# A new written order for five engines: the transposes of the second x0 half ahead of K's matmuls on the second kb slice, and the orders behind it

## The chip, the core and the metric

The kernel runs on one core of a Trainium2 chip. A core has TensorE (PE; its weight loads are shown apart as PEld), VectorE (DVE), ScalarE (ACT), GpSimd (POOL) and SyncE (SP), which here only issues DMAs. Each engine runs its own list of instructions in order, and the lists meet through semaphores. The metric is the device time of one execution in microseconds, median over runs. A profile is one execution; its span runs from the first to the last instruction of the program.

## What is computed

A gated sum of two branches over x of 2048 rows and 512 columns, in bf16. Branch a is attention with 32 heads of 16 columns, in four segments of 512 rows, with a running memory M, z that each segment reads and then extends. Branch b is a gated MLP with 1792 hidden columns.

```python
g = _sigmoid((x * gate_w).sum(-1, keepdims=True))
# branch a, segment s
logits = jnp.einsum('bhqd,bhkd->bhqk', qs, ks) * scale + mask
a_dot = jnp.einsum('bhqk,bhkd->bhqd', _softmax(logits), vs)
pq = phi(qs)
a_mem = num(pq, M) / den(pq, z)
o = sig_beta * a_mem + (1.0 - sig_beta) * a_dot
M, z = M + phi(ks).T @ vs, z + phi(ks).sum()
# branch b
h = _gelu(x @ w_gate) * (x @ w_up)
out = g * (o @ wo) + (1 - g) * (h @ w_down)
```

## The kernel before

The kernel is built from 1290 tasks, each a few instructions on one engine. The function `_build` makes them, `Sched.schedule` puts them in the order that the table `ORDER` (line 43) writes out for each engine, name by name, and `Emitter` adds the semaphore waits that follow from reads and writes. So the order on every engine is written by hand, or rather by a search that ran elsewhere, and the choice of engine for a task that can run on ScalarE or on VectorE is made by the list in which its name stands. `schedule` also walks through the lists with estimated durations, and from that it only takes which of the four PSUM banks psW0 to psW3 a group of matmuls gets (`Grp`, `bank_free`); `LANDING` (line 39) holds the landing times that it assumes for the first loads. Estimates don't change an order.

What the names mean, for segment s (0 to 3) and tile t:

- `x0t0a_u`, `x0t0b_u`, `x0t1_u`: the first segment's x comes in two halves u (`x0_0`, `x0_1`, 256 KB each, by SP) and is transposed on TensorE (line 645): two transposes, two, and four for each half. `x0ev...` copies them out of PSUM into xT (lines 652 and 653).
- `K0_t.i`: eight matmuls of 256 columns each, one task each, with i = 0 and 1 on the first x half with the first two slices of wk (`w_wk0`, `w_wk1`, 128 KB each, by ACT's queue), 2 and 3 the same on the second half, 4 to 7 with `w_wk2`. In this order `K0_t.0` needs wk0, `K0_t.1` needs wk1, and `.2` and `.3` need the second x half.
- `Q`, `V`, `G` (gate), `U` (up), `D` (down and output projection) with `s_t.0` and `.2`: two matmuls of 512 columns each, into a bank of psW. `Kev`, `Qev`, `Vev`, `Gev` copy a finished bank out (line 563 on ScalarE, 566 on VectorE). Q of segment 0 uses the banks of psXALL instead. `R` are the D matmuls of segments 0 to 2 cut into four row tiles that run side by side.
- `kp`, `kl`: copies of K masked for two interleaved heads (kpad, klow; lines 777, 786, 763, 765).
- `qk s_t A0 B0 L A1 B1`: logits of four heads at a time into all four banks of psXALL (line 928); `exp` (line 934, ScalarE) reads all four, so the next qk waits for the exp and the next exp for the qk. `msk` (line 937, GpSimd) cuts off the masked part. There are 18 of these a segment, and the other work of TensorE stands between them, about five pairs of matmuls a gap.
- `pv`, `pvt`, `norm`: the product with V in column tiles, its transpose on VectorE (line 990), and four or five steps that divide and write oT (lines 1002 to 1010).
- `pke`, `pkc`, `pqe`, `pqc`: phi of K and of Q, an exp on ScalarE (line 745) and two steps on VectorE (748, 750). `pkT` are DMA transposes of phi(K), `mz`, `mzacc`, `mzbd` (lines 894 to 913) bring the memory up to date; `numx`, `num`, `numd`, `nump`, `numl` read it; `oTd` are DMA transposes of the result.
- `gelu` (lines 1048 and 1059), `Um` (line 1075, the product with up), `fin` (lines 1123 and 1125, the scaled output) and `out`, its DMA. `gmul`, `gsum`, `gexs`, `gts`: the gate g of a segment; a gsum on ScalarE is line 813.

A run of tasks between two qk that has a `pv` in it is put into column tiles as a whole (`Sched.column_runs`): each matmul there is four instructions that run side by side.

The order on TensorE around the change:

```python
"... x0t0a_0 x0t0b_0 x0t1_0 K0_2.0 K0_3.0 K0_0.0 K0_1.0 K0_0.1 x0t0a_1 "
"K0_3.1 x0t0b_1 x0t1_1 K0_1.1 K0_2.1 K0_3.2 K0_2.2 K0_1.2 K0_2.3 ..."
```

## Time and profile before

| what | us |
|---|---|
| median of 3 runs | 262.89 |
| lowest, highest | 262.35, 263.35 |
| the profiled execution | 262.34 |
| its span, first to last instruction | 261.1 |
| TensorE busy | 256.8 |
| ScalarE busy | 210.6 |
| VectorE busy | 186.7 |
| GpSimd busy | 106.1 |

The granted clock of TensorE is 1.0 in this execution. In the rows, a group has its line in the kernel, engine, operation, the tile written and those read, the shape and how often; then the start and the length, or the busy time and the mean of one. In square brackets stands how long the engine had been idle before it and what ended that. SPq and ACTq are DMA issues of those engines.

### The profile page before, as it was taken

Reading aid. Unit: us, or ns where it says so; the run is one execution under the profiler, and the core shown is the slowest. Engines: PE = TensorE matmul, PEld = TensorE weight load, DVE = VectorE, ACT = ScalarE, POOL = GpSimd, SP = SyncE. Lnnn points to the kernel's source line nnn. Section 1 sums busy time; section 2 is a strip of 40 time slices with the busy share of each in tenths; the row PEclk is TensorE's granted clock in tenths of the full one; section 3 lists DMA queues with packets and bytes.
Section 4 is the critical chain, followed back from the end, with each engine's and each line's share of the span. In section 5 each row is a group of like instructions: output and inputs, shape, how many; then the busy total and the mean of one; then the engine's idle time right before and its main releaser. Section 6 shows DMA issues by size and latency. Waiting matters only on the chain.

```text
span 261.1 us, 10363 instructions
## 1 busy us (share of the span) xinstructions
PE 256.8 (98%) x4646; PEld 126.6 (48%) x4646; DVE 186.7 (71%) x350; ACT 210.6 (81%) x187; POOL 106.1 (41%) x260
## 2 busy tenths in 40 slices
PE   7999999999999999999999999999999999999996
PEld 3644445345544664534554563554455444453454
DVE  1598988998999238999986115999999502598743
ACT  3789898999999988789877788888975877776722
POOL 8316574923001873163650217352280053436420
DMA  6951338922126744110005113302000300310002
GB/s 220 316 171 22 64 64 237 312 24 83 24 22 149 102 98 65 32 54 3 3 9 124 36 22 81 86 7 82 0 6 11 72 5 0 85 43 3 3 3 83
DMA packets 33100, 18.43 MB, mean 71 GB/s; under 512 B 21152, under 2 KB 32800, under 8 KB 33056
## 3 DMA queue, kind: packets, MB, share of 16 engines
q1 hardware_dynamic: 32224, 16.99, 27.8%
q8 instruction: 36, 0.59, 1.0%
q10 hardware_dynamic: 832, 0.79, 0.9%
q14 instruction: 8, 0.07, 0.1%
HBM read 9.84 MB, written 2.10 MB: 46 GB/s over the span
## 4 chain that ended last, share of the span: by engine, by line
PE 93%; DVE 3%; DMA 2%; issue 1%; ACT 0%; DVEq 0%
PE psW L543 35%; PE psW L545 25%; PE psW L1096 14%; PE psXALL L928 8%; PE psW L976 5%; DMA wk<-in_A_wk_dram 2%; PE psXALL L545 2%; PE psW L984 1%; PE psXALL L543 1%; PE psXALL L847 1%; PE psW L894 1%; DVE tb L990 1%; DVE phq L750 0%; DVE obf L1006 0%; DVE hT L566 0%
## 5 line engine op out<-in xcount | busy, mean ns | idle before, releaser
L934 ACT ACTIVATE pt<-psXALL 128x2048 bf16<-128x2048 f32 x64 | 120.1, 1876 | 24.7 <-PE psXALL L928 21.9
L937 POOL TENSOR_SCALAR_AFFINE_SELECT pt<-pt 128x256 bf16<-128x256 bf16 x128 | 58.6, 470 | 92.6 <-ACT pt L934 88.1
L1075 DVE TENSOR_TENSOR hT<-psW,hT 128x512 bf16<-128x512 f32 x56 | 37.0, 683 | 7.2 <-PE psW L543 5.3
L937 POOL TENSOR_SCALAR_AFFINE_SELECT ptl<-ptl 128x512 bf16<-128x512 bf16 x32 | 22.1, 689 | 45.0 <-ACT ptl L934 43.2
L1096 PE MATMUL psW<-wd,hT 32*128 32x512 bf16 x576 | 35.0, 374 | 0.0
L543 PE MATMUL psW<-xT,wu 128*128 128x512 bf16 x118 | 29.4, 381 | 0.1
L545 PE MATMUL psW<-xT,wg 128*32 128x512 bf16 x464 | 27.8, 380 | 0.0
L990 DVE STREAM_TRANSPOSE tb<-psW 128x512 f32<-128x512 f32 x32 | 22.5, 707 | 6.6 <-PE psW L984 6.5
L543 PE MATMUL psW<-xT,wg 128*128 128x512 bf16 x108 | 26.3, 380 | 0.3 <-DVE hT L566 0.3
L545 PE MATMUL psW<-xT,wu 128*32 128x512 bf16 x424 | 26.0, 380 | 0.0
L928 PE MATMUL psXALL<-qT,kpad 32*128 32x320 bf16 (+3 forms) x512 | 25.7, 272 | 0.2 <-ACT ptl L934 0.2
L1125 DVE TENSOR_SCALAR ost<-psW,omgt 128x512 bf16<-128x512 f32 x10 | 7.4, 748 | 23.3 <-PE psW L543 21.6
L1096 PEld LDWEIGHTS psW<-wd,hT 32*128 32x128 bf16 x576 | 18.8, 93 | 10.6
L1059 ACT ACTIVATE hT<-psW 128x512 bf16<-128x512 f32 x28 | 15.6, 598 | 7.6 <-PE psW L545 7.5
L928 PEld LDWEIGHTS psXALL<-qT,kpad 32*128 32x128 bf16 x512 | 8.6, 92 | 23.1 <-ACT pt L934 16.0
L976 PE MATMUL psW<-pt,vaug 128*17 128x192 bf16 (+3 forms) x512 | 19.3, 273 | 0.0
L934 ACT ACTIVATE ptl<-psXALL 128x2048 bf16<-128x2048 f32 x8 | 15.1, 1882 | 2.7 <-PE psXALL L928 2.6
L543 PEld LDWEIGHTS psW<-xT,wu 128*128 128x128 bf16 x118 | 10.1, 98 | 13.7 <-issue 2.7
L976 PEld LDWEIGHTS psW<-pt,vaug 128*17 128x17 bf16 x512 | 12.1, 91 | 9.4 <-issue 0.8
L545 PEld LDWEIGHTS psW<-xT,wg 128*32 128x32 bf16 x464 | 11.3, 97 | 10.5 <-issue 0.6
L834 POOL COPY exsT<-exs 32x4 f32<-32x4 f32 x64 | 14.1, 220 | 5.2 <-ACT exs L824 1.5
L543 PEld LDWEIGHTS psW<-xT,wg 128*128 128x128 bf16 x108 | 10.0, 98 | 12.7 <-issue 0.6
(124 smaller groups left out, 382.5 us busy)
## 6 DMA issues: line engine op xcount, KB each, us to landing
out_dram<-ost SPq DMA_DIRECT2D x15, 128.0 KB, 1.9
wg<-in_B_w_gate_dram SPq DMA_DIRECT2D x2, 896.0 KB, 7.2
wu<-in_B_w_up_dram SPq DMA_DIRECT2D x2, 896.0 KB, 6.6
...
hT<-in_A_x_dram SPq DMA_DIRECT2D x2, 256.0 KB, 3.5
...
```

What stands on the lines that cost most here:

```text
L543: return e.matmul(view(), lhsT, rhs, start=first, stop=last)
L545: r = e.matmul(view()[c:c + 32, :], lhsT[:, c:c + 32], rhs, start=first, stop=last, tile_position=(0, c))
L834: cross = task(f"exsT{s}", POOL, [Instr(lambda e, g=g, c=c: e.tensor_copy(exsT[sl][32 * g:32 * g + 32, c:16:4], exs[32 * c:32 * c + 32, s4 ...
L928: instrs.append(Instr(lambda e, g=g, lhs=lhs, rhs=rhs, c0=c0, ncol=ncol: e.matmul(X[g][:, c0:c0 + ncol], lhs(32 * g), rhs(32 * g), start=T ...
L934: exp_task(s, f"exp{s}_{t}{name}", [Instr(lambda e: e.activation(dst[:], XALL[:, :].rearrange("p (g c) -> p g c", g=4), ACTF.Exp, scale=AT ...
L937: task(f"msk{s}_{t}{name}", POOL, [Instr(lambda e, view=view, pat=pat, base=base: e.affine_select(out=view, in_=view, compare_op=ALU.is_ge ...
L976: instrs.append(Instr(lambda e, t=t, q=q, kb=kb, slot=slot, c0=c0: e.matmul(gp.f32()[32 * q:32 * q + 17, 128 * kb + 64:512], Vaug[sl][:, k ...
L990: task(f"pvt{s}_{t}_{j}", DVE, [Instr(lambda e: e.transpose(Tb[:, j, :], gp.f32()[:, :]), [gp.key], [("Tb", j)], 0.71)], grp=gp)
L1059: lambda e, g=g, ft=ft, s=s: e.activation(hT[s % 2][:, ft, :], g.f32()[:, :], ACTF.Gelu_apprx_tanh),
L1075: task(f"Um{s}_{ft}", DVE, [Instr(lambda e, g=g, ft=ft: e.tensor_tensor(hT[sl][:, ft, :], g.f32()[:, :], hT[sl][:, ft, :], ALU.mult), [g.k ...
L1096: return Instr(lambda e: e.matmul(gs[tile].f32()[:, :], a[32 * r:32 * r + 32, :], b[32 * r:32 * r + 32, :], start=False, stop=False, tile_ ...
L1125: DVE: [Instr(lambda e: e.tensor_scalar(ost[:], g.f32()[:, :], omgt[:, gt:gt + 1], None, ALU.mult), rd, wr, dve_t(512, ap=True))]}, grp=g))
```

## The change

Only the two tables differ. In `LANDING`, x0_0 goes from 3.95 to 3.8 and w_wk1 from 5.3 to 5.7. In `ORDER`, all tasks are the same, but they stand in another order on every engine behind the first few, and 44 of those that can run on either of ScalarE and VectorE change the engine: 24 go to ScalarE, 20 to VectorE. In segment 0 these are 13 and 9.

```diff
 LANDING = {
-    "x0_0": 3.95, "w_wk0": 4.15, "x0_1": 5.2, "w_wk1": 5.3, "w_wk2": 6.6, ...
+    "x0_0": 3.8, "w_wk0": 4.15, "x0_1": 5.2, "w_wk1": 5.7, "w_wk2": 6.6, ...
...
     "pe": (
-        "warm0 ... x0t0a_0 x0t0b_0 x0t1_0 K0_2.0 K0_3.0 K0_0.0 K0_1.0 K0_0.1 x0t0a_1 "
-        "K0_3.1 x0t0b_1 x0t1_1 K0_1.1 K0_2.1 K0_3.2 K0_2.2 K0_1.2 K0_2.3 K0_1.3 K0_0.2 K0_2.4 K0_0.3 K0_1.4 K0_2.5 "
-        "K0_0.4 K0_3.3 K0_3.4 K0_1.5 K0_0.5 K0_0.6 K0_0.7 K0_2.6 K0_1.6 Q0_0.0 K0_1.7 Q0_1.0 K0_2.7 Q0_2.0 Q0_3.0 "
-        "Q0_0.2 Q0_1.2 K0_3.5 K0_3.6 Q0_3.2 Q0_2.2 K0_3.7 G0_2.0 G0_2.2 qk0_0A0 V0_3.0 V0_1.0 V0_1.2 V0_3.2 V0_0.0 "
+        "warm0 ... x0t0a_0 x0t0b_0 x0t1_0 K0_2.0 K0_3.0 K0_0.0 K0_1.0 x0t0a_1 x0t0b_1 "
+        "x0t1_1 K0_2.1 K0_3.1 K0_0.1 K0_1.1 K0_2.2 K0_3.2 K0_1.2 K0_0.2 K0_2.3 K0_1.3 K0_2.4 K0_0.3 K0_1.4 K0_2.5 "
+        "K0_0.4 K0_3.3 K0_3.4 K0_1.5 K0_0.5 K0_0.6 K0_2.6 K0_0.7 K0_1.6 K0_2.7 K0_1.7 Q0_3.0 Q0_0.0 Q0_1.0 Q0_1.2 "
+        "Q0_0.2 Q0_2.0 Q0_3.2 Q0_2.2 K0_3.5 K0_3.6 K0_3.7 G0_2.0 G0_3.0 qk0_0A0 G0_2.2 V0_2.0 V0_3.0 V0_3.2 V0_2.2 "
...
-        "qk0_2L G0_10.2 G1_3.0 G1_4.0 G1_4.2 G1_3.2 qk0_2A1 G0_1.0 G1_0.0 G0_1.2 G1_0.2 K1_3.0 qk0_2B1 G0_11.0 K1_3.2 "
+        "mz0 qk0_2L G0_0.0 V1_3.0 G1_4.0 G1_4.2 G0_0.2 qk0_2A1 G1_3.0 G1_3.2 V1_3.2 G0_10.0 G0_10.2 qk0_2B1 G0_11.0 "
...
     "act": (
-        "tload w_wk0 w_wk1 w_wq0 w_wv0 x0ev0b_0 x0ev0b_1 x0ev1_1 K0_0even K0_0ev K0_1ev pke0_0 kl0_11 Q0_1ev Q0_3ev "
-        "K0_3ev exp0_0A0 Vev0_1 gexp exp0_0B0 Vev0_0 Vev0_2 exp0_0L kl0_30 exp0_0A1 Vev1_1 exp0_0B1 pke0_1 exp0_1A0 "
+        "tload w_wk0 w_wk1 w_wq0 w_wv0 x0ev0b_0 x0ev0b_1 x0ev1_1 K0_0even K0_1ev K0_2ev kl0_01 pke0_0 Q0_1ev Q0_0ev "
+        "Q0_3ev kl0_10 K0_3ev exp0_0A0 gexp Vev0_3 exp0_0B0 gsum0_1 kl0_20 exp0_0L Vev0_0 exp0_0A1 Gev0_7 exp0_0B1 "
...
-        "exp1_2B0 exp1_2L K2_1ev exp1_2A1 exp1_2B1 pqe2_1 exp1_3A0 gsum2_1 exp1_3B0 gsum2_0 gsum2_2 exp1_3A1 Vev2_3 "
+        "exp1_2A0 Vev2_0 fin0_3 exp1_2B0 Q2_2ev exp1_2L pqe2_1 exp1_2A1 exp1_2B1 exp1_3A0 K2_0ev exp1_3B0 gsum2_3 "
+        "gsum2_0 gsum2_2 exp1_3A1 Vev2_3 gexs2 exp1_3B1 gelu2_0 gelu2_1 gelu2_2 gelu2_3 gelu2_4 gelu2_5 gelu2_6 "
...
     "dve": (
-        "x0ev0a_0 x0ev0a_1 x0ev1_0 kl0_01 K0_2ev kl0_10 Q0_0ev kp0_0 kl0_00 Q0_2ev Gev0_2 kp0_1 gmul0 kl0_31 Vev0_3 "
+        "x0ev0a_0 x0ev1_0 x0ev0a_1 K0_0ev kp0_0 kl0_21 kp0_1 Q0_2ev gmul0 Gev0_2 gsum0_2 kl0_11 Vev0_2 kl0_00 gsum0_3 "
...
-        "Gev1_9 pqc1_0 pvt0_1_0 mzacc0 Gev0_10 pvt0_1_1 mzbd0 Gev1_3 pqc1_1 Gev0_1 norm0_1 K1_3ev Gev0_11 gmul1 "
+        "pvt0_1_1 pvt0_1_0 mzacc0 pqc1_1 norm0_1 Vev1_3 Gev0_10 gmul1 Gev0_1 gsum1_0 gsum1_1 gsum1_2 mzbd0 K1_3ev "
...
     "pool": (
-        "ident masks vones consts msk0_0B0 msk0_0A0 omg msk0_0L msk0_0B1 msk0_0A1 exsT0 msk0_1A1 msk0_1B0 msk0_1A0 "
+        "ident masks vones msk0_0B0 msk0_0A0 msk0_0L msk0_0A1 msk0_0B1 exsT0 omg msk0_1A1 msk0_1A0 msk0_1B1 msk0_1B0 "
...
     "sp": (
-        "x0_0 x0_1 w_wk2 w_wq1 w_wv1 w_wg0 x1_0 w_gwb x1_1 w_beta x1_2 x1_3 w_wg1 Vlo0_0 gl10 gl11 gl00 gl01 pkT0_0 "
-        "Vlo0_1 pkT0_2 pkT0_1 pkT0_3 x2_3 x2_2 w_wu1 xt1 w_wu0 w_wd0 x2_0 x2_1 w_wo Vlo1_1 oTd1_2 oTd1_3 oTd1_1 w_wd1 "
+        "x0_0 x0_1 w_wk2 w_wq1 w_wv1 w_wg0 x1_0 w_gwb x1_1 w_beta x1_2 x1_3 w_wg1 gl00 gl11 Vlo0_1 gl10 gl01 pkT0_1 "
+        "pkT0_0 Vlo0_0 pkT0_2 pkT0_3 xt1 x2_3 x2_0 w_wu0 x2_1 w_wd0 w_wu1 w_wd1 x2_2 w_wo oTd1_0 x3_2 oTd1_1 oTd1_2 "
```

In the last segments the lists move in the same way: D1_3.16 goes behind qk2_1A1, fin1_0 from ScalarE to VectorE, and at the end ScalarE has fin3_1 and VectorE fin3_2 and fin3_0, where ScalarE had fin3_0 and fin3_2 and VectorE fin3_1.

More of the change, by code (lines that the diff above doesn't have):

```diff
@@ L39 @@
 LANDING = {
-    "x0_0": 3.95, "w_wk0": 4.15, "x0_1": 5.2, "w_wk1": 5.3, "w_wk2": 6.6, "w_wq0": 7.0, "w_wq1": 8.4, "w_wv0": 9.2,
+    "x0_0": 3.8, "w_wk0": 4.15, "x0_1": 5.2, "w_wk1": 5.7, "w_wk2": 6.6, "w_wq0": 7.0, "w_wq1": 8.4, "w_wv0": 9.2,
     "w_wv1": 10.2, "w_wg0": 12.2, "x1_0": 12.9, "w_gwb": 13.2, "x1_1": 13.8, "w_beta": 14.1, "x1_2": 14.4, "x1_3": 14.8,
```

147 rows, old and new, of the table ORDER are left out of this document.

## The prediction

> **What bounds the kernel now.** I read the shares of the page first, then the busy time by stretches of the span, then the chain of waits, and last the rows around its few waits.
>
> ```profile
> PE 256.8 (98%) x4646; PEld 126.6 (48%) x4646; DVE 186.7 (71%) x350; ACT 210.6 (81%) x187; POOL 106.1 (41%) x260
> PE 93%; DVE 3%; DMA 2%; issue 1%; ACT 0%; DVEq 0%
> ```
>
> ```profile
> 4.00:21.50 17.50, 16.71 (x146) 8.70 (x143) 11.59 (x25) 13.39 (x19) 7.44 (x19) 1.00 0.81 231
> 21.50:58.70 37.20, 36.92 (x589) 16.61 (x588) 33.92 (x62) 33.98 (x31) 22.29 (x55) 1.00 0.54 125
> 58.70:203.00 144.30, 144.26 (x2843) 72.73 (x2843) 111.06 (x213) 123.97 (x114) 54.20 (x134) 1.00 0.24 50
> 203.00:258.60 55.60, 55.23 (x1044) 27.10 (x1046) 29.76 (x52) 37.43 (x24) 19.35 (x40) 1.00 0.10 25
> ```
>
> The columns of the stretches are: length, then busy time of PE, PEld, DVE, ACT and POOL, then clock, DMA share and GB/s. TensorE is the bound in every stretch: it idles 0.79 us (17.50 less 16.71), then 0.28, 0.04 and 0.37, together 1.48 us between 4 and 258.6 us. Ends of matmuls are modelled, so gaps under some 0.27 us hide in "busy"; but what an order can win is of the size of 1.5 us, 0.6% of the time. VectorE (33.92 of 37.20) and ScalarE (33.98) are close behind in the second stretch: there a task put on the wrong one of the two can cost TensorE time.
>
> The 0.79 us has two parts at the start:
>
> ```profile
> 4.61 0.61 PE L543 MATMUL psW<-xT,wk 128*128 128x256 bf16 x4 [0.21 <-DVE xT L653]
> 5.80 0.27 PE L543 MATMUL psW<-xT,wk 128*128 128x256 bf16 x1 [0.58 <-DMA wk<-in_A_wk_dram]
> 5.91 0.27 PE L645 MATMUL psXALL<-ident,hT 128*128 128x128 bf16 x2
> 6.02 0.27 PE L543 MATMUL psW<-xT,wk 128*128 128x256 bf16 x1
> 6.13 0.50 PE L645 MATMUL psXALL<-ident,hT 128*128 128x128 bf16 x6
> 6.46 2.51 PE L543 MATMUL psW<-xT,wk 128*128 128x256 bf16 x21
> ```
>
> K0_0.1 stands ahead of the transposes of the second half of x0 and waits for wk1, so the transposes wait with it. The second wait that shows is at 48.43 us:
>
> ```profile
> 45.07 0.72 DVE mzbd L913
> 46.31 0.42 DVE phq L748
> 46.76 1.02 DVE phq L750
> 47.77 0.61 DVE hT L566
> 48.43 0.61 PE psW L543 x2
> ```
>
> These are steps of the chain of waits: G0_11.0 needs one of the four psW banks, and the copy that frees it (L566, Gev0_1) stands on VectorE behind mzbd0 and pqc1_1, both of which took long.
>
> **The head.** The order of the DMA issues at the start is unchanged, so the landings stay where they were.
>
> ```profile
> 1.27 0.42 SPq L580 DMA_DIRECT2D hT<-in_A_x_dram  x1
> 1.73 0.43 SPq L580 DMA_DIRECT2D wk<-in_A_wk_dram  x1
> ```
>
> ```profile
> hT<-in_A_x_dram SPq DMA_DIRECT2D x1, 256.0 KB, 4.1
> wk<-in_A_wk_dram SPq DMA_DIRECT2D x1, 256.0 KB, 5.3
> ```
>
> ```profile
> 1.29 4.37 DMA wk<-in_A_wk_dram
> ```
>
> x0's second half lands at 1.27 + 4.1 = 5.4 us, wk1 at 1.29 + 4.37 = 5.66, wk2 at 1.73 + 5.3 = 7.0. The diff puts all eight transposes of that half (x0t0a_1, x0t0b_1, x0t1_1) ahead of K0_2.1. They can start at 5.46 instead of 5.91. Six of them took 0.50 us with a last one of 0.22 (rows above), 0.056 us apart, so eight take 0.45 us and end at 5.91. The four matmuls K0_t.1 then issue back to back, 0.11 us each (21 in 2.51 - 0.27 us, the rows of 6.46), to 6.35. The same work was over at 6.72 before (both remaining K0_t.1 after 6.46, and a small gap). That is 0.37 us sooner. VectorE's copies follow: x0ev1_0 now stands before x0ev0a_1, but its transposes are done at 4.4, so it runs in the idle time before 5.3 and delays nobody. Then K0_2.4 needs wk2: six matmuls stand ahead of it, so TensorE is there at 6.35 + 6 x 0.11 = 7.01, against the landing at 7.0 plus the 0.13 us from landing to matmul that wk1 shows (5.66 to 5.80): 0.12 us back. What TensorE carries on is 0.25 us.
>
> In a sentence that the sum doesn't need: the Trainium skill, TensorE: Matmul & The Clock Gate, PE-mode transpose, says that transposes do not count as busy for the clock gate and stay at half rate; by that the eight would take 0.45 us more and the head would be about 0.1 us slower than before. The rows above deny it here: 0.056 us apart right behind an idle 0.58 us, at clock 1.00.
>
> **What ScalarE makes of the head.** The next consumer is exp0_0A0, behind these:
>
> ```profile
> 8.86 0.69 ACT L734 ACTIVATE kpad<-psW,maskc 128x512 bf16<-128x512 f32 x1 [1.36 <-PE psW L543]
> 9.57 1.09 ACT L563 ACTIVATE kT<-psW 128x512 bf16<-128x512 f32 x2
> 10.69 1.06 ACT L745 ACTIVATE pex<-kT 128x1024 bf16<-128x1024 bf16 x1
> 11.65 0.57 ACT L763 ACTIVATE klow<-kT,maskc 128x256 bf16<-128x256 bf16 x1
> 12.09 1.05 ACT L563 ACTIVATE qT<-psXALL 128x512 bf16<-128x512 f32 x2
> 13.03 0.59 ACT L563 ACTIVATE kT<-psW 128x512 bf16<-128x512 f32 x1
> 14.22 1.88 ACT L934 ACTIVATE pt<-psXALL 128x2048 bf16<-128x2048 f32 x1 [0.59 <-PE psXALL L928]
> 16.81 1.88 ACT L934 ACTIVATE pt<-psXALL 128x2048 bf16<-128x2048 f32 x1
> ...
> 47.58 0.60 ACT L563 ACTIVATE hT<-psW 128x512 bf16<-128x512 f32 x1
> ```
>
> ```profile
> 18.95 0.41 PE L928 MATMUL psXALL<-qT,klow 32*128 32x64 bf16 x32
> ...
> 21.56 0.40 PE L928 MATMUL psXALL<-qT,kpad 32*128 32x448 bf16 x8
> ```
>
> Before, ScalarE had 0.59 us to spare there. Now its list ahead of exp0_0A0 is K0_0even, three copies that were two (K1, K2 for K0, K1), kl0_01, pke0_0, three copies of Q that were two, kl0_10, K0_3ev: from start to start 0.71 + 2 x 0.50 + 0.48 + 0.96 + 3 x 0.48 + 0.44 + 0.50 = 5.5 us. K0_0even follows K0_0.7, which is eleven matmuls behind K0_2.4 (7.13 + 11 x 0.11 = 8.33; before it was 18 behind the one at 6.46, 8.48), so it starts 0.15 us sooner, at 8.71, so exp0_0A0 starts at 14.2: where it was. TensorE reaches qk0_0A0 at 13.51 for 13.77, but the next qk0_0B0 writes the same four psXALL banks and waits for exp0_0A0's end at 16.1. Behind exp0_0B0 stand gsum0_1 and kl0_20 (1.05 us, for two copies of 0.85), so exp0_0L is late by about 0.3 us, and qk0_0A1, which came 2.61 us after qk0_0L (18.95 and 21.56), waits 0.15. From qk0_0B0 at 16.23 (16.10 and the 0.13 that a release takes) two such steps and the wait give qk0_0A1 at 21.6 us, against 21.56. **Head, net: 0.0 us.** Bounds: -0.37 if ScalarE's copies run closer together than I take them, +0.25 if one more of them (0.5 us) stands out by half.
>
> **The bank wait at 48.4 us.** mzbd0 now stands behind mzacc0 with nine tasks between them instead of two on VectorE, and VectorE has four tasks fewer before 61 us (thirteen go to ScalarE, nine come back: among them Gev0_7, 0_11, 0_12, 1_3, 1_9, Vev0_3). The bank that G0_11.0 wants is now freed by ScalarE, with the copy right behind exp0_2A1: the row at 47.58 stands in that place and ends at 48.18. G0_11.0 comes at about 48.3, since one more pair of matmuls (0.43 us) stands before it and the present wait (0.42 us: the 0.28 of idle time that VectorE's row shows at 48.43 and what the modelled ends hide) is not there. The wait goes, with 0.1 us to spare. The five further copies on ScalarE (0.5 us each) fall into gaps between exps of 0.72 us, two in one gap in two places, where TensorE waits some 0.05 us each time. **-0.31.** Bounds -0.42 and 0.
>
> The reason why the margin matters:
>
> ```profile
> L750 DVE TENSOR_TENSOR phq<-phq,pex 128x1024 bf16<-128x1024 bf16 x6 | 4.6, 760 | 1.8 <-ACT pex L745 1.6
> L913 DVE TENSOR_TENSOR mzbd<-blkm,mzc 128x136 bf16<-128x136 bf16 x3 | 1.3, 444 | 0.1
> 45.05 3.23 POOL L937 TENSOR_SCALAR_AFFINE_SELECT ptl<-ptl 128x512 bf16<-128x512 bf16 x4 [2.91 <-ACT ptl L934]
> ```
>
> The L750 at 46.76 took 1.02 us while its five fellows average (6 x 760 - 1016) / 5 = 709 ns, the L913 at 45.07 took 0.72 for 0.31; both ran under GpSimd's selects of 45.05 to 48.28. So 0.3 to 0.4 us is what such a meeting adds to a VectorE step that reads two SBUF tiles.
>
> **Later stages.** The number of changes between full and tiled matmuls is 156 in both orders and the matmuls are the same, so TensorE's own work is equal. Behind exp1_3B0 ScalarE gets three gsums for two:
>
> ```profile
> 121.10 0.62 ACT L813 ACTIVATE phkt<-phkt 128x512 bf16<-128x512 bf16 x1
> ```
>
> ```profile
> L1125 DVE TENSOR_SCALAR ost<-psW,omgt 128x512 bf16<-128x512 f32 x10 | 7.4, 748 | 23.3 <-PE psW L543 21.6
> ```
>
> Three of them less one overlap take 1.73 us in a gap of 0.72: exp1_3A1 is 1.0 us late, and TensorE, though it has 0.56 us more work between the two qk now, waits 0.23 us, where two gsums made it wait some 0.1: **+0.12**, bounds 0 and +0.62. fin1_0 goes to VectorE, where fin1_0, 1_1 and 1_2 (0.75 us each) now follow one another; U2_13.0 wants the bank of the third some 0.1 us before it is free: **+0.1**, bounds 0 and +0.75. At the end two of the last fins follow on VectorE and the last outputs queue on SP: **+0.05**, bounds 0 and +0.3. The loads of x2, wu, wd, wo change places on SP; by the issue times each still lands over 3 us ahead of its first reader: 0.
>
> **Sum**: 0.0 - 0.31 + 0.12 + 0.1 + 0.05 = -0.04 us on the profiled execution of 262.34 us (span 261.1 and 1.2 outside it), 262.3. That execution stands 0.55 us under the median of the three runs, so in runs like those: 262.89 - 0.04, about **262.8 us**. No change.
>
> **Rivals.**
> 1. *The head's gain stays and the bank wait goes*: ScalarE's list is shorter than I take it, exp0_0A0 starts at 13.9, and nothing new comes: -0.37 - 0.42 = -0.8, **262.1 us**. For it: TensorE is the bound, ScalarE had 0.59 us spare at 14.2. Against: it has one copy and one klow more there.
> 2. *The transposes aren't ahead of anything*: the two landings are 0.24 us apart, and where x0's half lands behind wk1, K0_t.1 wait behind transposes that wait. As much later as x0 then is: 0.2 us for a landing at 5.9, and the bank wait stays: **263.1 us**. Against: the issue order is unchanged.
> 3. *Slower: banks freed late behind VectorE*. The searched order leaves margins of 0.1 us at psW banks (48.3 us above). Where a step with two SBUF inputs meets a GpSimd select, the copy behind it frees its bank 0.3 to 0.4 us late, and TensorE waits as at 48.4: 0.42 us each. The select order is new, and VectorE runs such steps (L750, L1006, L1010, L913) in all segments. It decides from four such waits: 4 x 0.42 - 0.04 = +1.6, **264.5 us**. Against: today's order has the same steps and one such wait in 144 + 37 us; for it: the steps meet at new places, and the order was spread by times in which every wait is as small as it gets. The Trainium skill, SBUF — State Buffer, Two separate sides, says that VectorE with two SBUF inputs and a GpSimd operation that reads SBUF exclude each other for the whole instruction; the two long rows agree with it.
>
> **How the numbers follow.** Chances: forecast 0.57 (own range 262.2 to 263.4, from the scatter of 1.0 us in the three runs), rival 1 0.15, rival 2 0.08, rival 3 0.20. 0.5% is 1.3 us, about what a measurement tells from no change. Faster than 261.58 takes nearly all of the 1.48 us of idle time: about half of rival 1 with a low run, 0.07. Slower than 264.2: most of rival 3 and a little of the rest, 0.18. Within: 0.75. The range goes from 261.7 (rival 1 less 0.4 of scatter) to 264.3 (three or four bank waits).
>
> **What would show it.** Head: transposes back to back from 5.46, K0_2.1 at 5.91, K0_2.4 behind wk2 at 7.1, exp0_0A0 still at 14.2 and qk0_0A1 at 21.6. Bank: no gap of TensorE at 48 us. Later: a gap of about 0.2 us ahead of qk1_3B1. Wrong would be: exp0_0A0 at 13.9 (rival 1), the transposes later than 5.6 (rival 2), or idle times of TensorE released by VectorE of 0.3 us or more in several places between 20 and 203 us (rival 3).

## The result, and the profile after

| | before | after |
|---|---|---|
| median, us | 262.64 (261.89 to 263.35, 15 runs) | 261.68 (261.07 to 262.15, 15 runs) |
| the profiled execution | 262.34 | 261.81 |
| its span | 261.1 | 260.6 |

The ratio is 0.9964, with an interval of 0.9953 to 0.9976: the changed kernel is 0.96 us faster, 0.36%. Forecast was 262.8 us and no change.

The busy times and the chain of waits, of the profile after:

```profile
PE 256.8 (99%) x4670; PEld 127.1 (49%) x4670; DVE 186.6 (72%) x346; ACT 211.3 (81%) x191; POOL 105.9 (41%) x260
PE 96%; DMA 2%; ACT 1%; SPq 0%; issue 0%; DVE 0%
```

VectorE is gone from the chain (3% before), TensorE has 96% of it for 93%. TensorE has 24 matmuls and 24 weight loads more than before (4670 for 4646). The stretches, with the same columns as in the prediction:

```profile
4.00:21.50 17.50, 17.02 (x146) 9.15 (x144) 11.71 (x23) 13.97 (x22) 5.66 (x8) 1.00 0.81 228
21.50:58.70 37.20, 37.20 (x598) 16.54 (x597) 33.13 (x63) 35.55 (x33) 24.03 (x64) 1.00 0.51 138
58.70:203.00 144.30, 144.26 (x2834) 72.96 (x2831) 109.78 (x208) 123.36 (x113) 54.62 (x136) 1.00 0.24 46
203.00:258.60 55.60, 55.20 (x1093) 27.32 (x1090) 31.66 (x55) 36.95 (x23) 18.70 (x40) 1.00 0.12 32
```

TensorE idles 0.48 us in the first stretch (0.79 before), none in the second (0.28), and 0.04 and 0.40 in the others. That is 0.56 us less than before, and the two profiled executions differ by 0.53; but the agreement is partly chance. 0.31 of the 0.56 lies in the first stretch, and there exp0_0A0, the first exp, starts at 14.22 us before and after: the first eight transposes took 1.01 us for 0.62, which counts as busy. What the change won lies further on, in part in waits that no row shows as idle. ScalarE is busier in the second stretch (35.55 for 33.98 us), VectorE less (33.13 for 33.92).

TensorE and ScalarE in the head after, and three steps of the chain there (start, length, what):

```profile
5.20 0.61 PE L645 MATMUL psXALL<-ident,hT 128*128 128x128 bf16 x8
5.64 1.25 PE L543 MATMUL psW<-xT,wk 128*128 128x256 bf16 x10
7.38 1.81 PE L543 MATMUL psW<-xT,wk 128*128 128x256 bf16 x15 [0.48 <-DMA wk<-in_A_wk_dram]
```

```profile
8.96 0.69 ACT L734 ACTIVATE kpad<-psW,maskc 128x512 bf16<-128x512 f32 x1 [2.29 <-PE psW L543]
11.88 1.58 ACT L563 ACTIVATE qT<-psXALL 128x512 bf16<-128x512 f32 x3
14.22 1.91 ACT L934 ACTIVATE pt<-psXALL 128x2048 bf16<-128x2048 f32 x1
```

```profile
1.72 5.61 DMA wk<-in_A_wk_dram
7.38 1.81 PE psW L543 x15
9.19 3.45 PE psXALL L543 x16
```

The transposes run back to back, from 5.20, and K0_2.1 follows at 5.64. Ten matmuls on, TensorE stands still until wk2 lands, in this execution at 1.72 + 5.61 = 7.33 us, 0.33 later than in the one before. So exp0_0A0 starts at 14.22, to the hundredth where it was, and as forecast; but for another reason, as the runs below show. From wk2's landing on, TensorE is never out of the chain in the head: ScalarE's longer list isn't in it, though it runs into exp0_0A0 without a gap where it had 0.59 us to spare before.

The place of the bank wait, TensorE and ScalarE after:

```profile
48.14 0.40 PE L928 MATMUL psXALL<-qT,kpad 32*128 32x320 bf16 x8
48.47 1.90 PE L543 MATMUL psW<-xT,wg 128*128 128x512 bf16 x8
```

```profile
47.77 0.59 ACT L563 ACTIVATE hT<-psW 128x512 bf16<-128x512 f32 x1
```

The matmuls follow the logits after 0.33 us, the least that these rows show; the copy that frees the bank is ScalarE's and ends at 48.36.

Where the rest of the gain is, VectorE and GpSimd around 232 us, first before, then after:

```profile
232.47 0.91 DVE L1006 TENSOR_TENSOR obf<-tb,sc 128x512 bf16<-128x512 f32 x1
234.25 0.51 DVE L1010 TENSOR_TENSOR oT<-oT,ott 128x512 bf16<-128x512 bf16 x1
234.69 0.68 DVE L1075 TENSOR_TENSOR hT<-psW,hT 128x512 bf16<-128x512 f32 x1
232.42 2.08 POOL L937 TENSOR_SCALAR_AFFINE_SELECT pt<-pt 128x256 bf16<-128x256 bf16 x4 [4.91 <-ACT pt L934]
```

```profile
232.07 0.69 DVE L1006 TENSOR_TENSOR obf<-tb,sc 128x512 bf16<-128x512 f32 x1
233.65 0.42 DVE L1010 TENSOR_TENSOR oT<-oT,ott 128x512 bf16<-128x512 bf16 x1
233.99 0.68 DVE L1075 TENSOR_TENSOR hT<-psW,hT 128x512 bf16<-128x512 f32 x1
234.53 2.84 POOL L937 TENSOR_SCALAR_AFFINE_SELECT ptl<-ptl 128x512 bf16<-128x512 bf16 x4 [3.98 <-ACT ptl L934]
```

Before, the multiply of norm3_0 (L1006) and its last step (L1010) began under four selects: the two of msk3_2B0 and, behind them in GpSimd's list, the two of msk3_2A0. After, msk3_2A0 no longer stands behind msk3_2B0 and is done by 230.6 us, msk3_2B0 comes later, and the two VectorE steps are 0.31 us shorter together. The next step, L1075, frees the psW bank that TensorE wants: at 235.37 us before, at 234.67 after. TensorE behind it, before and then after:

```profile
234.93 0.40 PE L928 MATMUL psXALL<-qT,kpad 32*128 32x448 bf16 x8 [0.18 <-ACT ptl L934]
235.43 2.33 PE L543 MATMUL psW<-xT,wu 128*128 128x512 bf16 x10
```

```profile
234.52 0.40 PE L928 MATMUL psXALL<-qT,kpad 32*128 32x448 bf16 x8 [0.18 <-ACT ptl L934]
234.85 2.33 PE L543 MATMUL psW<-xT,wu 128*128 128x512 bf16 x10
```

From the logits to the next matmul it is 0.50 us before and 0.33 after: a wait of 0.17 that no row shows as idle, since the modelled end of the logits covers it.

**Head and body.** In what follows the span is cut at the start of exp0_0A0, the first row of L934 on ScalarE. The part from there to the start of the last scaling step (fin3_31, L1162 on VectorE) is called the body: 259.14 - 14.22 = 244.92 us before, 258.53 - 14.22 = 244.31 after, **-0.61**. It came out the same in four executions with the changed body (-0.61 and three times -0.59), and to the hundredth in two with the body of before. Two others had a loss of 0.1 and 0.2 us on top, and the run page one of 1.5, all told below; so one profile tells bodies apart by some 0.2 us, and mostly by less. What varies is the head: exp0_0A0 starts between 13.76 and 14.60 us in the executions profiled.

### The profile page after: what moved, and what is told of

It is laid out like the page before. It is cut to its first block, busy times and chain, and to the rows that moved or that the text cites. A ratio compares the mean times of both kernels' runs of the same rounds, so it can differ in the third digit from the quotient of the medians.

```text
span 260.6 us, 10413 instructions
## 1 busy us (share of the span) xinstructions
PE 256.8 (99%) x4670; PEld 127.1 (49%) x4670; DVE 186.6 (72%) x346; ACT 211.3 (81%) x191; POOL 105.9 (41%) x260
## 4 chain that ended last, share of the span: by engine, by line
PE 96%; DMA 2%; ACT 1%; SPq 0%; issue 0%; DVE 0%
PE psW L543 36%; PE psW L545 26%; PE psW L1096 14%; PE psXALL L928 9%; PE psW L976 6%; DMA wk<-in_A_wk_dram 2%; PE psXALL L545 2%; PE psW L984 1%; PE psXALL L543 1%; ACT ptl L934 1%; PE psXALL L847 1%; PE psW L894 1%; SPq L580 0%; DVE obf L1162 0%
## 5 line engine op out<-in xcount | busy, mean ns | idle before, releaser
L934 ACT ACTIVATE pt<-psXALL 128x2048 bf16<-128x2048 f32 x64 | 120.1, 1877 | 24.5 <-PE psXALL L928 23.5
L937 POOL TENSOR_SCALAR_AFFINE_SELECT pt<-pt 128x256 bf16<-128x256 bf16 x128 | 56.1, 448 | 90.4 <-ACT pt L934 85.6
L937 POOL TENSOR_SCALAR_AFFINE_SELECT ptl<-ptl 128x512 bf16<-128x512 bf16 x32 | 23.9, 748 | 48.6 <-ACT ptl L934 47.0
L1075 DVE TENSOR_TENSOR hT<-psW,hT 128x512 bf16<-128x512 f32 x56 | 37.2, 684 | 8.8 <-PE psW L543 6.7
L543 PE MATMUL psW<-xT,wg 128*128 128x512 bf16 x128 | 31.3, 380 | 0.0
L543 PE MATMUL psW<-xT,wu 128*128 128x512 bf16 x126 | 31.3, 380 | 0.0
L545 PE MATMUL psW<-xT,wu 128*32 128x512 bf16 x392 | 24.6, 380 | 0.0
L1125 DVE TENSOR_SCALAR ost<-psW,omgt 128x512 bf16<-128x512 f32 x11 | 8.0, 746 | 23.1 <-PE psW L543 21.9
L545 PE MATMUL psW<-xT,wg 128*32 128x512 bf16 x384 | 22.9, 379 | 0.0
L543 PEld LDWEIGHTS psW<-xT,wg 128*128 128x128 bf16 x128 | 11.5, 98 | 14.4 <-issue 1.5
L543 PEld LDWEIGHTS psW<-xT,wu 128*128 128x128 bf16 x126 | 11.2, 98 | 14.3 <-issue 2.1
L934 ACT ACTIVATE ptl<-psXALL 128x2048 bf16<-128x2048 f32 x8 | 15.0, 1877 | 1.6 <-PE psXALL L928 1.6
L545 PEld LDWEIGHTS psW<-xT,wu 128*32 128x32 bf16 x392 | 10.1, 97 | 9.5 <-issue 0.8
```

Of the source, the lines that this page charges most:

```text
L543: return e.matmul(view(), lhsT, rhs, start=first, stop=last)
L545: r = e.matmul(view()[c:c + 32, :], lhsT[:, c:c + 32], rhs, start=first, stop=last, tile_position=(0, c))
L934: exp_task(s, f"exp{s}_{t}{name}", [Instr(lambda e: e.activation(dst[:], XALL[:, :].rearrange("p (g c) -> p g c", g=4), ACTF.Exp, scale=AT ...
L937: task(f"msk{s}_{t}{name}", POOL, [Instr(lambda e, view=view, pat=pat, base=base: e.affine_select(out=view, in_=view, compare_op=ALU.is_ge ...
L1075: task(f"Um{s}_{ft}", DVE, [Instr(lambda e, g=g, ft=ft: e.tensor_tensor(hT[sl][:, ft, :], g.f32()[:, :], hT[sl][:, ft, :], ALU.mult), [g.k ...
L1125: DVE: [Instr(lambda e: e.tensor_scalar(ost[:], g.f32()[:, :], omgt[:, gt:gt + 1], None, ALU.mult), rd, wr, dve_t(512, ap=True))]}, grp=g))
```

## The experiments

All tables of bodies are against the 244.92 us of the kernel before. Line numbers of L543 to L1162 are one or two higher in some of these kernels.

**One place at a time.** Two kernels take the kernel before and change one place.

```diff
 "pe":  (head)
-"... K0_1.0 K0_0.1 x0t0a_1 K0_3.1 x0t0b_1 x0t1_1 K0_1.1 K0_2.1 ..."
+"... K0_1.0 x0t0a_1 x0t0b_1 x0t1_1 K0_0.1 K0_3.1 K0_1.1 K0_2.1 ..."
 "dve": (head)
-"x0ev0a_0 x0ev0a_1 x0ev1_0 ..."
+"x0ev0a_0 x0ev1_0 x0ev0a_1 ..."
 "dve": (bank)
-"... mzbd0 Gev1_3 pqc1_1 Gev0_1 norm0_1 ..."
+"... mzbd0 Gev1_3 Gev0_1 pqc1_1 norm0_1 ..."
```

> The kernel before with one edit: on TensorE the transposes of the second x0 half stand ahead of K0_0.1, on VectorE x0ev1_0 stands ahead of x0ev0a_1. ScalarE's list is the old one, with 0.59 us to spare ahead of exp0_0A0. Theory A (the head is worth nothing in the change only because ScalarE's longer list ahead of exp0_0A0 takes it back; the profiled gain of 0.6 us is all of it from the later bank wait and from the last segment): here the 0.25 us that TensorE keeps goes through, exp0_0A0 at 13.9 to 14.0 us, time 0.25 us under the kernel before, ratio 0.999. Theory B (the loads of the start land at other times from execution to execution, and the old order waits for a late wk1 with the transposes behind it; this is the part of the measured 0.96 us that the two profiles don't show): 0.4 to 0.6 us under it, ratio 0.998. If ratio 1.000, the head is worth nothing with either list.

> The kernel before with one edit: on VectorE Gev0_1, which frees the psW bank that G0_11.0 waits for, stands ahead of pqc1_1 instead of behind it. Theories A and B alike: TensorE's gap of 0.42 us at 48 us is gone, and as nothing takes it back the time is 0.36 us under the kernel before, ratio 0.9986. If ScalarE's chain of gelus (exp0_3B1 to exp1_0A0, back to back) were the bound there, 0.1 us or less.

head: 262.29 us, ratio 0.9992 (0.9981 to 1.0003), body 0.00. Its interval holds theory A and no change alike, and its profile decides nothing on the head: wk2 landed at 7.53 us there, K0_2.4 followed at 7.58 and exp0_0A0 at 14.44. bank: 262.82, ratio 1.0008 (0.9995 to 1.002), body +0.16, where both theories had -0.36. In bank the wait at 48 us is gone, but VectorE shows a new one, and TensorE others behind it:

```profile
47.38 0.69 DVE L567 CAST hT<-psW 128x512 bf16<-128x512 f32 x1 [0.61 <-PE psW L544]
...
51.06 2.55 PE L544 MATMUL psW<-xT,wg 128*128 128x512 bf16 x10
...
56.39 0.40 PE L929 MATMUL psXALL<-qT,kpad 32*128 32x448 bf16 x8
56.85 1.44 PE L544 MATMUL psW<-xT,wg 128*128 128x512 bf16 x5
```

Ten matmuls take 2.55 us where ten without a wait take 2.33 (the run bank_relief below), and 0.46 us lie between the logits and the next matmul instead of 0.33; a further wait of 0.19 is inside the last row. In its new place Gev0_1 has VectorE wait 0.61 us for the matmuls that it copies, with pqc1_1 standing behind it, and the copies that follow come some 0.7 us later, counted from exp0_0A0: the place alone is worth nothing.

**Which part of the order.** Two kernels splice the orders at 61 us: seg0_after has the changed kernel's orders up to there and those of before behind, rest_after the other way round.

```diff
 each list of ORDER (seg0_after)
-tasks that start before 61 us, in the order of before
+the same tasks in the changed order
...
 each list of ORDER (rest_after)
-tasks that start behind 61 us, in the order of before
+the same tasks in the changed order
```

> All engines in the order of the changed kernel for what starts before 61 us there (head and segment 0), and in the order of the kernel before from there on. Theory A: the bank wait alone, 0.36 us under the kernel before, ratio 0.9986. Theory B: the head's 0.4 to 0.6 us as well, 0.7 to 0.9 us under it, ratio 0.997.

> The other way round: the order of the kernel before for what starts before 61 us, that of the changed kernel from there on. Theory A: what segment 0 doesn't explain, 0.25 us by the profiles (VectorE steps at 231 to 235 us) and up to 0.6 us by the runs, ratio 0.998. Theory B: 0.25 us, ratio 0.999.

seg0_after: 262.14 us, ratio 0.9991 (0.9973 to 1.0008), body 0.00. rest_after: 263.94, ratio 1.0053 (1.0035 to 1.0072), body +1.38. Neither number is the worth of its half, because the seam makes waits of its own: in seg0_after TensorE waits 0.24 us for a copy of ScalarE's ahead of 60.87 us, and in rest_after:

```profile
64.93 1.48 PE L547 MATMUL psW<-xT,wu 128*32 128x512 bf16 x24 [0.76 <-ACT kT L565]
```

In seg0_after exp0_3B1 is 0.72 us sooner than before, counted from exp0_0A0, its logits on TensorE 0.39, and exp1_0B0 level. rest_after shows one usable thing: between exp1_0B0 (+1.63) and the end (+1.38) it wins 0.25, so the later segments hold a gain of that size. A third kernel asked whether ScalarE's longer chain at the seam is the cause: seg0_after with the copy Gev1_1 moved from ScalarE to VectorE behind Um0_2.

```diff
 "act":
-"... gelu0_2 Gev1_1 gelu0_6 ..."
+"... gelu0_2 gelu0_6 ..."
 "dve":
-"... Um0_2 nump1_1 ..."
+"... Um0_2 Gev1_1 nump1_1 ..."
```

> The kernel of seg0_after with one task moved: Gev1_1 from ScalarE to VectorE, behind Um0_2. In seg0_after the 0.72 us that segment 0 had won at exp0_3B1 shrank to 0.11 at exp1_0A0 and to 0 at qk1_0B0, since ScalarE ran 19.2 us there without a gap for 18.6 before (one copy more, Gev1_1 beside Gev0_13). If ScalarE's chain of gelus is the bound of that stage, exp1_0A0 is 0.6 to 0.7 us ahead of the kernel before (counted from qk0_0A0) and qk1_0B0 0.35 us. If TensorE or VectorE is the bound, qk1_0B0 stays where it was.

262.40 us in one execution; exp1_0A0 came 0.60 us sooner than in the kernel before, as forecast for a bound by ScalarE, but exp1_0B0 stayed at +0.06. ScalarE's chain is not the only bound there, and the seam stayed unexplained.

**The changed kernel again, and without parts of its head.** after2 is the changed kernel. after_oldhead puts the old places of the transposes and of x0ev1_0 back. wk2_alone issues wq0 and wv0 behind wk2 on SP, so that wk2 shares the DMA engines with less.

```diff
 "pe":  (after_oldhead)
-"... K0_1.0 x0t0a_1 x0t0b_1 x0t1_1 K0_2.1 K0_3.1 K0_0.1 K0_1.1 K0_2.2 ..."
+"... K0_1.0 K0_0.1 x0t0a_1 K0_3.1 x0t0b_1 x0t1_1 K0_1.1 K0_2.1 K0_2.2 ..."
 "dve": (after_oldhead)
-"x0ev0a_0 x0ev1_0 x0ev0a_1 ..."
+"x0ev0a_0 x0ev0a_1 x0ev1_0 ..."
 "act": (wk2_alone)
-"tload w_wk0 w_wk1 w_wq0 w_wv0 x0ev0b_0 ..."
+"tload w_wk0 w_wk1 x0ev0b_0 ..."
 "sp":  (wk2_alone)
-"x0_0 x0_1 w_wk2 w_wq1 w_wv1 ..."
+"x0_0 x0_1 w_wk2 w_wq0 w_wq1 w_wv0 w_wv1 ..."
```

> The changed kernel once more, as the mark for the next two. Two claims are at stake. Claim 1: from qk0_0A0 on, an order takes the same time in every execution (the four orders that share the old list of segment 0 agreed to 0.01 us up to 46 us), so here fin3_31 starts 244.76 us behind qk0_0A0 as in the first profile, and only the head moves, with the landings of x0's second half, wk1 and wk2. Claim 2: K0_2.4 follows wk2's landing by 0.05 to 0.15 us or x0's second half by 1.6 us, whichever is later, and qk0_0A0 follows K0_2.4 by 6.38 us in every order. If ScalarE's longer list took the head's gain back, as forecast, qk0_0A0 would come at 13.7 or later even with wk2 landed by 6.6.

> The changed kernel with TensorE's old order up to K0_2.1 (K0_0.1 ahead of the transposes) and VectorE's old order of the first three copies; all behind is as changed. Theory H (the head is worth what the two profiles don't show of the measured 0.96 us): 0.3 to 0.4 us over after2; body 244.76 us as there. Theory S (the head is worth nothing in the median, the unshown part is chance): the same as after2 within 0.15 us.

> The changed kernel, with w_wq0 and w_wv0 issued by SP behind w_wk2 instead of by ScalarE's queue beside it: less is in flight beside wk2. If wk2's landing is what the changed head most often waits for, wk2 lands at 6.3 to 6.6 us for 7.3, K0_2.4 starts at 6.9 to 7.0, and the time is 0.2 to 0.4 us under after2. If x0's second half is what binds, it is the same as after2. If wq0 now lands behind 9 us, Q0 waits for it and it is slower.

after2: 261.67 us, ratio 0.997 (0.9959 to 0.9981). after_oldhead: 261.87, ratio 0.9972 (0.9961 to 0.9983): 0.20 us over after2 by the medians, 0.11 by the means, which decides neither for theory H nor for theory S. wk2_alone: 261.62, ratio 0.9965 (0.9949 to 0.998). All three bodies are -0.59. In wk2_alone wk2 landed at 5.82 us, and the head was still no shorter in the profiled execution (exp0_0A0 at 14.37), for a reason that TensorE's rows show:

```profile
5.63 0.98 PE L646 MATMUL psXALL<-ident,hT 128*128 128x128 bf16 x8
6.45 2.02 PE L544 MATMUL psW<-xT,wk 128*128 128x256 bf16 x17
```

The eight transposes took 0.98 us here, 0.107 us apart, and 0.61 in the profile after, 0.056 apart: TensorE was still at about half rate when they ran.

**The two gains of the body, rebuilt on the kernel before.** bank_relief is bank with one copy less on VectorE. pool3 moves one select.

```diff
 "dve": (bank_relief, besides bank's edit)
-"... gmul1 Gev0_12 gsum1_0 ..."
+"... gmul1 gsum1_0 ..."
 "act": (bank_relief)
-"... exp0_2B1 Gev1_4 exp0_3A0 ..."
+"... exp0_2B1 Gev1_4 Gev0_12 exp0_3A0 ..."
 "pool": (pool3)
-"... msk3_2B0 msk3_2A0 msk3_2L msk3_2B1 ..."
+"... msk3_2A0 msk3_2L msk3_2B0 msk3_2B1 ..."
```

> The kernel of the run bank (before with the copy Gev0_1 ahead of pqc1_1 on VectorE) with the copy Gev0_12 taken from VectorE and put on ScalarE behind Gev1_4. Theory (the gain of segment 0 needs both: the copy ahead of the long step, and VectorE relieved of a copy of 0.6 us, since otherwise the copies behind it are late one after the other): no gap at 48 us, and the waits of 0.2 us at 51.5 and of 0.39 us in all at 56.4 are gone or under 0.1 together; the logits qk1_0B0 come 0.25 to 0.4 us sooner after exp0_0A0 than in the kernel before. Rival (the waits further on come from GpSimd's selects or from the order of the matmuls, which stay as before): the waits at 51.5 and 56.4 stay at 0.3 us or more in all, and qk1_0B0 comes where it came in bank, +0.16 us, or no sooner than -0.1.

> Kernel before, but on GpSimd the select of 3_2B0 stands behind that of 3_2L, as in the changed kernel; nothing else moves. Theory (the changed select order takes GpSimd out of the way of the norm's two long VectorE steps, and with it the gap ahead of the projection matmuls near 235 us): L1006 near 232 us takes 0.69 instead of 0.91 us, L1010 near 234 us 0.42 instead of 0.51, TensorE's wait of 0.24 us there falls to about 0.07, and from exp0_0A0 to the end the kernel takes 0.15 to 0.2 us less than before. Rival (the gap comes from TensorE's own order around the logits of 3_2A1, which is also changed): the VectorE steps may shorten, but the wait stays at 0.2 us or more and the body at -0.05 to +0.05.

bank_relief, one execution: 261.62 us, body **-0.32**, of it -0.31 by exp1_0B0. The same places as in bank:

```profile
50.31 2.33 PE L544 MATMUL psW<-xT,wg 128*128 128x512 bf16 x10
...
55.42 0.40 PE L929 MATMUL psXALL<-qT,kpad 32*128 32x448 bf16 x8
55.75 2.38 PE L544 MATMUL psW<-xT,wg 128*128 128x512 bf16 x10
```

All three waits are gone. pool3, one execution: 261.82 us, body **-0.19**, all of it at 235 us:

```profile
232.09 0.69 DVE L1007 TENSOR_TENSOR obf<-tb,sc 128x512 bf16<-128x512 f32 x1
233.66 0.43 DVE L1011 TENSOR_TENSOR oT<-oT,ott 128x512 bf16<-128x512 bf16 x1
```

```profile
234.55 0.40 PE L929 MATMUL psXALL<-qT,kpad 32*128 32x448 bf16 x8 [0.18 <-ACT ptl L935]
234.88 2.33 PE L544 MATMUL psW<-xT,wu 128*128 128x512 bf16 x10
```

The VectorE steps have the changed kernel's lengths, and TensorE goes on after 0.33 us. That is the step from the select to the gain, with nothing else moved: the theory held in both runs, and both rivals fell. Each is one execution, but parts below shows both gains again at the same places: -0.32 us by exp1_0B0, and -0.18 between exp3_2L and exp3_2B1.

**The head once more, and the sum of the parts.** head_again repeats head. parts is the kernel before with the edits of head, bank_relief and pool3 together.

> The run head once more (before, with only the transposes of the second x0 half ahead of K0_0.1 on TensorE and x0ev1_0 ahead of x0ev0a_1 on VectorE), since its first interval, 0.9981 to 1.0003, holds both what the forecast said of the head and what the medians less the bodies say. Theory (the transposes ahead are worth 0.2 to 0.4 us in the median of the executions): ratio 0.9985 to 0.9992. Rival (they are worth nothing, the forecast's 0.0, and the gain of the changed kernel's head is by the draw of the executions or by its other moves): 0.9996 to 1.0004. In either case the body from exp0_0A0 to the end is that of before to 0.02 us.

> The kernel before with four small edits alone: the transposes of the second x0 half ahead of K0_0.1 with x0ev1_0 ahead of x0ev0a_1 (as in head), Gev0_1 ahead of pqc1_1 and Gev0_12 on ScalarE behind Gev1_4 (as in bank_relief), msk3_2B0 behind msk3_2L (as in pool3). Theory (these places are where the change gains, and their gains add): from exp0_0A0 to the end -0.31 - 0.19 = -0.50 us, and -0.25 in the head, -0.75 in all: ratio 0.9965 to 0.9978, against 0.9964 and 0.997 for the changed kernel. Rival 1 (the head's order is worth nothing): the same body, ratio 0.9979 to 0.9985. Rival 2 (gains of different places don't add, a gap moves on): body no better than -0.35.

head_again: 262.44 us, ratio 0.9997 (0.9984 to 1.0011): the rival's value. Its body was not that of before, as both had expected, but +0.20: Q2_2.0 came 0.19 late at 103.8 us, in an execution in which the output and the x load issued at 99.6 and 100.0 took 3.7 and 3.8 us to land (1.9 and 2.6 before). Whether the one caused the other stays open. parts: 262.04, ratio **0.9974** (0.9962 to 0.9987), inside the theory's range. Its body was -0.38, with a loss of 0.11 at 91.6 us that none of its parts shows in its own profile; without it, -0.49, where -0.31 - 0.19 = -0.50 was expected. The gains of the places add.

**What is left.** The changed kernel still waits for the exp behind qk3_2L (the 0.18 in its row at 234.52), since only four pairs of matmuls stand there. shift puts a fifth pair there by moving five qk back; pv_late moves pv3_1_1 there.

```diff
 "pe": (shift; 2B1, 3A0, 3B0 and 3A1 likewise one task later)
-"... U3_2.0 U3_2.2 qk3_2A1 U3_1.0 U3_1.2 ..."
+"... U3_2.0 U3_2.2 U3_1.0 qk3_2A1 U3_1.2 ..."
 "pe": (pv_late)
-"... pv3_1_0 pv3_1_1 qk3_2L U3_4.0 ..."
+"... pv3_1_0 qk3_2L pv3_1_1 U3_4.0 ..."
```

> The changed kernel, with qk3_2A1, 2B1, 3A0, 3B0 and 3A1 each one matmul pair later in TensorE's list, so that the stretch behind qk3_2L holds five pairs instead of four and the later ones keep their count. Theory (what TensorE still waits for at 234.3 us is the exp of qk3_2L, whose stretch is too short): the gap of 0.18 us in the row there goes, -0.2 to -0.25 us from exp0_0A0 to the end, median some 0.2 us below the changed kernel's, ratio to before about 0.9955. Rival (the logits that come later make the last exps and with them the last norm late): the gap goes, but pv3_3_1 or the last norm waits as much more at the end: 0.0, ratio 0.9965.

> The changed kernel with pv3_1_1 behind qk3_2L instead of ahead of it in TensorE's list. Its bank is there and VectorE wants its result only at 239 us, so that it can fill the stretch behind qk3_2L, which has four pairs and waits for exp3_2L. Theory (the wait at 234 us is the exp's, and the stretch lacks work that needs no bank of VectorE's): qk3_2L comes some 0.4 us sooner, exp3_2L then follows fin2_3 at once, the gap of 0.18 us at 234.3 is under 0.05, and the body is 0.1 to 0.2 us shorter than the changed kernel's: ratio 0.9955 to 0.9965. Rival (TensorE then waits ahead of qk3_2L for exp3_2B0, or ScalarE for fin2_3, and the gap moves there): body within 0.05 of the changed kernel's.

shift: 262.27 us, ratio 0.9994 (0.9979 to 1.0008), body -0.14, 0.47 worse than the changed kernel. Both theories missed what came:

```profile
234.75 0.61 PE L544 MATMUL psW<-xT,wu 128*128 128x512 bf16 x2 [0.40 <-DVE hT L1076]
```

The fifth pair needs a bank that VectorE frees late, and now the logits stand behind that wait, at 235.29 us for 234.52. pv_late: 263.32, ratio 1.0029 (1.0014 to 1.0045). The theory's gain did not come, and the body (-0.46) is 0.15 worse than the changed kernel's, more than the rival had. The cause is a third one: exp3_2L overwrites what pv3_1_1 reads, and waits for it:

```profile
232.52 1.88 ACT L935 ACTIVATE ptl<-psXALL 128x2048 bf16<-128x2048 f32 x1 [0.62 <-PE psW L985]
```

But the time is some 1.6 us above the changed kernel's, and that much is lost behind the start of the last scaling step: 263.39 - 258.45 = 4.94 us, against 261.81 - 258.53 = 3.28 in the profile after. DMA issues of SP in that profile, the last one 2.04 us long for 0.45 after:

```profile
258.38 0.45 SPq L581 DMA_DIRECT2D out_dram<-pex  x1
258.88 2.04 SPq L581 DMA_DIRECT2D out_dram<-obf  x1
```

pv_late has 24 more matmuls on TensorE than the changed kernel (4694 weight loads for 4670, one for each matmul; some matmuls are missing from that profile), because the pairs behind qk3_2L now run in column tiles. page has these 24 in another way: three of the seven warm-up matmuls at the start are cut into nine of 64 columns each, and nothing else is moved.

```diff
-        task(f"warm{i}", PE, [Instr(lambda e, gw=gw: e.matmul(
-            gw.f32()[:, :], ones[:, 0:128], ones[:, :], start=True, stop=True),
-            [], [gw.key], mm_t(512))], grp=gw, bias=5000.0 - i)
+        n = 64 if i in (3, 4, 5) else 512
+        task(f"warm{i}", PE, [Instr(lambda e, gw=gw, n=n: e.matmul(
+            gw.f32()[:, 0:n], ones[:, 0:128], ones[:, 0:n], start=True, stop=True),
+            [], [gw.key], mm_t(n)) for _ in range(9 if n == 64 else 1)], grp=gw, bias=5000.0 - i)
```

> The changed kernel with three of the seven warm-up matmuls of 512 columns at the start cut into nine of 64 columns each: 24 more instructions on TensorE, as in pv_late, and nothing else. Theory (the count moves the fetch of TensorE's last instructions to the time of the outputs, and the outputs wait behind it): 58 fetches of instructions instead of 57, the last at about 259 us, the last outputs land 3.2 to 3.8 us after their issue instead of 1.6 to 1.8, and the time is 1.3 to 1.8 us above the changed kernel's: ratio to before 1.001 to 1.005. Rival (the loss of pv_late comes from its move): the body as in the changed kernel, outputs at 1.6 to 1.8 us, ratio 0.996 to 0.9985, with up to 0.3 us from a later end of the warm-up.

page: **264.91 us**, ratio 1.0095 (1.0077 to 1.0114), worse than the theory had it. Its DMA queues from 256 us on (packets, MB, share; then KB and us from issue to landing):

```profile
q8 instruction: 1, 0.02, 1.0%
...
out_dram<-pex SPq DMA_DIRECT2D x1, 96.0 KB, 3.2
out_dram<-obf SPq DMA_DIRECT2D x1, 32.0 KB, 2.9
```

The same view of the profile after has no instruction packet there:

```profile
out_dram<-pex SPq DMA_DIRECT2D x1, 96.0 KB, 1.8
out_dram<-obf SPq DMA_DIRECT2D x1, 32.0 KB, 1.6
```

From the start of the last scaling step to the end it is 264.92 - 260.34 = 4.58 us, against 3.28 in the profile after: +1.30. So 24 more matmuls at the start are enough to make the end late, as the theory had it; that the outputs wait behind the fetch is read from the times at which they fall, and not shown by itself. The theory missed that the body would lose 1.51 as well, in places where TensorE waits for nothing that the profile shows, the largest here:

```profile
111.17 0.61 PE L545 MATMUL psW<-xT,wu 128*32 128x512 bf16 x6 [0.62 <-issue]
```

No version was found that beats the changed kernel.

## Why the prediction was wrong

By its own terms, forecast against measured:

| step | forecast | measured |
|---|---|---|
| head | 0.0 | some -0.3 |
| bank wait at 48.4 us | -0.31 | -0.36 by exp1_0B0 |
| three gsums behind exp1_3B0 | +0.12 | 0 |
| fin1_0 on VectorE (whole of segment 2) | +0.1 | -0.04 |
| selects of 3_2, not forecast | | -0.18 |
| tail | +0.05 | -0.03 in the body, some +0.04 behind it |
| sum | -0.04 | -0.96 in the medians |

The body's lines are the times of the exps after exp0_0A0, after against before: -0.36 at exp1_0B0, -0.36 at exp2_0A0, -0.40 at exp3_0A0, -0.58 at exp3_2B1, -0.61 at the end. What lies behind the start of the last scaling step isn't in the body: 3.20 us before and 3.28 after, and on average 3.23 in the nine profiled executions with the tail of before and 3.27 in six with the changed one.

Of the 0.92 us between -0.04 and -0.96, the head is about 0.3, the three added costs some 0.3, the selects 0.18 and the bank wait 0.05. A further 0.25 us of the way from 262.8 to 261.68 us is the starting point: the median of before was 262.89 in three runs and is 262.64 in fifteen.

**The step that failed is "Head, net: 0.0 us".** The prediction had the transposes 0.37 us sooner, gave 0.12 back to wk2, and let ScalarE's longer list take the other 0.25: "so exp0_0A0 starts at 14.2: where it was". The third number was wrong. ScalarE's list did not hold exp0_0A0 back: the logits qk0_0A0 came 6.38 us after K0_2.4 before (7.39 to 13.77), after (7.38 to 13.77) and in seg0_after (6.93 to 13.31), and exp0_0A0 started 0.45 us behind them in all three, whether ScalarE had 0.59 us to spare or nothing. With the longer list and wk2 landed at 6.52 us, exp0_0A0 was there at 13.76 in seg0_after. The list from K0_0even to exp0_0A0 takes 5.25 us (8.51 to 13.76) and not 5.5; nearly half of the error is K0_0even, taken as 0.71 us from rows in which the next copy began only behind its end, and 0.59 after (8.96 to 9.55). The list just fits, and what K0_2.4 wins, exp0_0A0 wins.

The second number, 0.12 for wk2, is that of one execution. In the profile after, wk2's later landing took the whole gain, and the 14.22 forecast came true by coincidence. In six of the eleven profiled executions with the transposes ahead (after, after2, head, seg0_gev, shift, page) K0_2.4 follows wk2's landing by 0.04 to 0.05 us; the old order, which had K0_2.4 1.72 us behind wk1's landing (5.67 to 7.39 before), would by that estimate have been in time for it as well. In three more (head_again, parts, wk2_alone) the transposes ran at about half rate.

**How much the head is worth** can't be read from one execution, since its landings vary; so it is the difference of the medians less the body's. This remainder holds what lies behind the body too. For the five kernels with the changed head as a whole (the changed kernel, after2, wk2_alone, seg0_after, shift) it is -0.35, -0.35, -0.40, -0.35 and -0.09, weighted by their 58 executions -0.30. With the transposes alone (head, head_again with the body of before, parts) it is -0.20, -0.06 and -0.07, mean -0.11 over 36 executions (head_again's own body would make its -0.06 a -0.26); with the other new lists and the old transposes (after_oldhead) -0.15 over 11; with the head of before (bank, rest_after) +0.17 and +0.07. One execution scatters by some 0.35 us, so each of these is good to 0.1 to 0.2; means in place of medians give -0.24 for the whole head and -0.15 for the transposes. That the head as a whole gains is shown by these times; how it is shared between the transposes, which give the change its name, and the other lists is not settled. The profiles don't settle it either: exp0_0A0 starts at 14.05 us on average in six executions with the whole head as changed, at 14.21 in five with the head of before and at 14.43 in three with the transposes alone, and single ones differ by up to 0.8. One execution shows a part of the lists: in bank_relief, which has the lists of before, K0_2.4 started at 6.86 and qk0_0A0 at 13.38, which is 6.52 us and not 6.38, with 0.13 us lost ahead of G0_2.0 at 12.4; in seg0_after, nearly as early, nothing was lost.

**The sum** of body and head, -0.61 - 0.30 = -0.91, is close to the measured -0.96; in part it has to be, since the changed kernel's own times are among those that the head's -0.30 is read from.

**The bank wait** went as forecast, and for the reason given: "VectorE has four tasks fewer". The freeing copy is ScalarE's and ends at 48.36 us, 0.11 ahead of the matmuls, where 48.18 and a margin of 0.1 were forecast. On the kernel before, bank and bank_relief show that the relief of VectorE was the condition, and that the copy's place alone gives the gain back at 51 and 56 us.

**The added costs** of +0.27 were not there. The third gsum does make exp1_3A1 late (+0.20 against before, where exp1_2A0 stands at -0.35), but TensorE has six groups of work between that qk and the next, and the last of them ends just ahead of the next logits:

```profile
123.50 0.29 PE L984 MATMUL psW<-ptl,vlow 128*17 128x64 bf16 x16
123.83 0.40 PE L928 MATMUL psXALL<-qT,kpad 32*128 32x320 bf16 x8
```

What TensorE waits there, some 0.1 us, it waited before as well. fin1_0's segment brought a small gain, and the tail about nothing. The prediction took it that a later step makes TensorE later; at exp1_3A1 there was work of TensorE's between, and that it was so for fin1_0 too is not shown by a row.

**The rivals.** Rival 1 (head gain stays, bank wait goes, 262.1) was nearest, and its argument, that ScalarE had 0.59 us to spare, was the better one; but it lacked the selects, its sign (exp0_0A0 at 13.9) didn't show in the profile after, and its -0.37 for the transposes is more than the runs give them. Rival 2 fell: the x0 half landed 0.18 to 0.33 us ahead of wk1 in every profiled execution, and the transposes ran ahead. Rival 3 had its mechanism right and its sign wrong: VectorE steps do meet selects, and the changed order took such a meeting away (pool3). The Trainium skill, SBUF — State Buffer, Two separate sides, which the prediction cited for it, has one engine wait for the whole instruction of the other; pool3 agrees: without the meeting L1006 is 0.22 us shorter and L1010 0.08, each less than one select (2.08 / 4 = 0.52 us).

The statement that "TensorE's own work is equal" was wrong in the count, by 24 matmuls. That cost nothing that shows here, but page has 24 more again, and is 3.2 us slower than the changed kernel.
